# Attention pairs in eight slots: the steps of one turn taken from four different pairs

## The chip, the cores and the metric

The kernel runs on one core of a Trainium2 chip. Its metric is the device time of one execution in microseconds (us); for the kernel before, the median of three timed runs is 537.44 us (534.42 to 538.1).

## What is computed

Attention over 8 batches, 12 heads, 448 positions and 64 dimensions per head feeds a mixture of 8 experts, in which each expert takes at most 80 tokens:

```python
scores = scale * np.matmul(q, k.transpose(0, 1, 3, 2))
scores = np.where(mask, -1000000000.0, scores)          # causal
attn = np.exp(scores - np.max(scores, axis=-1, keepdims=True))
attn = attn / (np.sum(attn, axis=-1, keepdims=True) + 1e-09)
x = np.matmul(attn, v)                                  # -> rows of 768
logits = x @ w_gate; expert_idx = np.argmax(logits, axis=1)
for e in range(8):
    tok_idx = ...    # the 80 tokens of e with the largest gate weight
    out[tok_idx] = gate_w[tok_idx, None] * (np.maximum(x[tok_idx] @ w1[e], 0.0) @ w2[e])
```

## The kernel before, in words

**Pairs.** The attention runs over 48 pairs of heads, six to a batch. A pair's queries are cut into seven tiles (t = 0 to 6) of 64 queries for each of the two heads, one head in the lower 64 partitions and one in the upper. Tile t meets 64(t+1) keys. For a pair the kernel does, in this order:

- *scores*: two groups of TensorE (PE) matmuls (`products`, L355) into PSUM tiles `sp`. Group s0 holds tile 6 (one bank) and tiles 5 and 0 (a second bank); s1 holds tiles 4 and 1, 3 and 2. There are three `sp` banks, so four banks a pair go round three buffers.
- *softmax* of each tile (`softmax`, L358): the maximum, one VectorE (DVE) instruction that also scales and masks (`ns`, `nb`, L362), called m6, m5, ... below; and the exponential on ScalarE (ACT) into `prob` (L365), called e6, e5, ...
- *transposes*: two groups (`transpose_groups`, L379) of 16 PE instructions, t0 and t1, into the one two-bank PSUM tile `tp`, each with an ACT copy of that tile into `PT` (L384), c0 and c1. Since there is one `tp` buffer, t1 waits for c0 and the next t0 waits for c1. Group 0 reads all seven tiles of the pair, so t0 waits for the last exponential.
- *values*: 32 PE matmuls over four chunks of keys (`values_group`, L405) into the one `xp` bank, then a DVE copy into `xu` (L411).

**The order.** Everything in the attention is issued in the order that the program writes (`tc.manual_schedule()`, L891), and each engine works through its own instructions in that order. The loop of L911 gives each pair i eight slots. Slot by slot it puts the scores and softmax of pair i, the transposes of pair i-1 and the values of pair i-2 (`SCORES`, `TURNS`, `VALUES`, `READ` and `SOFT`, L27 to L28). On PE a turn so reads s0, t0, s1, t1, values; on ACT e6 e5 e0, c0, e4 e1 e3 e2, c1; on DVE the seven maxima, then the copy to `xu`.

**Batch steps.** When six pairs are done, the batch's other work is spread over the slots of later pairs by tables of slot numbers (`ROWS0`, `ROWS1`, `STEPS`, `batch_plan`, L871): transposes of the result rows (`rt`, L505) with a DVE scaling (L524) and a DMA to `xs`, the gate product (`gp`, L457), its transposes (`lp`), and the selection of each expert's best 80 tokens (`selt`, `rn`, `rl`, `cp`, `gt`, `tn` on PE, `less`, `lt`, `rm`, `rr` on DVE). Batch 6 has a table of its own (`EARLY`), and the last batch runs in `TAIL` (L39), after the pairs. These PE steps take PSUM from `ps_m`, two banks under one tag.

After the tail the experts run (L1255 on). The SP queue loads q and k half a batch ahead (three pairs), loads v, writes zeros to the output and loads the first expert weights in slots 1, 4 and 7.

Of the kernel before, what the change touches and what calls it, by code (L numbers as in the profile page):

```python
# [7 lines left out]
F32 = mybir.dt.float32  # L8
# [9 lines left out]
P = 128  # L18
# [4 lines left out]
TILES = 7  # L23
# [3 lines left out]
SCORES, TURNS, VALUES, READ = (0, 2), (1, 4), 5, 6  # L27
SOFT = {0: [6], 1: [5, 0], 2: [4], 3: [1, 3], 4: [2]}  # L28
# [11 lines left out]
u ta ya v0 tb yb v1 turned vy guard invert placed w gp0 wy close piece gp1 gs  # L40
# [8 lines left out]
def attention_then_moe(  # L49
# [13 lines left out]
    B, _, NP, S = qT.shape  # L63
# [5 lines left out]
    NT = (S + P - 1) // P  # L69
# [16 lines left out]
    apool = att.enter_context(tc.tile_pool(name="att", bufs=2))  # L86
# [36 lines left out]
    WIDTH = [QB * (t + 1) for t in range(TILES)]  # L123
# [210 lines left out]
    def scores_groups(pr, n):  # L334
# [32 lines left out]
        return products, softmax  # L367
# [482 lines left out]
    pairs = []  # L850
# [40 lines left out]
    with tc.manual_schedule():  # L891
# [18 lines left out]
        parts = []  # L910
        for i, pr in enumerate(pairs):  # L911
# [12 lines left out]
            products, softmax = scores_groups(pr, i)  # L924
            turns = transpose_groups(pairs[i - 1]) if i else []
            values = values_group(pairs[i - 2]) if i >= 2 else None
            for k in range(SLOTS):
                if k in SCORES:
                    products(SCORES.index(k))
                if turns and k in TURNS:  # L930
                    turns[TURNS.index(k)][0]()
                if values and k == VALUES:
                    values[0]()
                for t in SOFT.get(k, []):
                    softmax(t)
                if turns and k in TURNS:
                    turns[TURNS.index(k)][1]()
                if values and k == READ:
                    values[1]()
                for f in plan.pop(i * SLOTS + k, []):  # L940
                    f()

                if i == n - PH and k == 4 and len(wload) >= WBUF and not parts:
                    load_piece()

                if i > 4 and k in (1, 4, 7):
                    if not parts and len(wload) < WBUF:
                        parts = piece_parts()
                    if parts:
                        parts.pop(0)()  # L950
                    elif zdone[0] < N:
                        zero_rows()
# [25 lines left out]
        steps["u"] = lambda: None  # L978
# [357 lines left out]
```

## Time and profile before

| what | value |
| --- | --- |
| median of three runs | 537.44 us |
| the profiled execution | 536.23 us |
| its span, first to last instruction | 534.5 us |
| attention, from the first scores to the last transposes | 4.6 to 386 us |
| tail of the last batch and start of the experts | 386 to 425 us |
| experts | 425 to 534.5 us |
| busy: PE, PE weight loads, ACT, DVE | 454.5, 356.9, 372.2, 355.7 us |
| mean granted TensorE clock | 0.972 |

The profile gives busy time per engine, the granted clock of TensorE (1.0 is 2.4 GHz, 0.5 is 1.2 GHz), who waited for whom, and the chain of waits: the work that ended last, followed back step by step to whatever released it. In the attention the same picture repeats with every batch of six pairs, about 48.5 us, so a batch and a single pair are the units to read.

### The profile page before, as it was taken

The page shows a single profiled execution, that of the slowest core. Times are in us where ns is not written, and L with a number is a line of the kernel's source. Part 1 is how long each engine was busy: PE and PEld are TensorE (multiplying, and loading weights), DVE is VectorE, ACT ScalarE, POOL GpSimd, SP SyncE. Part 2 cuts the span into 40 slices and gives each one's busy share as a digit, 9 for nine tenths or more (in the row PEclk, how much of TensorE's full clock was granted, in tenths as well). Part 3 has the DMA queues.
Part 4 walks back from the last instruction along what each step waited for, and adds up shares of the span by engine and source line. Part 5 has one row for each costly group of instructions (what it writes and reads, how often), then busy time and mean ns, then how long its engine had stood idle before and what let it go on. Part 6 is the DMA issues. An engine that isn't in the chain of part 4 may idle for free.

```text
span 534.5 us, 17567 instructions
## 1 busy us (share of the span) xinstructions
PE 454.5 (85%) x7093; PEld 356.9 (67%) x7093; DVE 355.7 (67%) x1224; ACT 372.2 (70%) x973; POOL 79.6 (15%) x211
## 2 busy tenths in 40 slices
PE   5778878798788888787987888788887999999995
PEld 2556556556566566565565656666664999999994
DVE  4455465576566656765765567567756499999883
ACT  5876776767756847667667486575757399988792
POOL 4201010101101010101011001101045014522001
PEclk9899899999999989999999999999999599999998
DMA  7416595375559345842745360426164599999931
GB/s 259 171 53 221 164 326 184 103 238 178 197 166 324 109 148 169 286 160 107 254 164 186 120 243 21 169 75 215 25 268 149 174 394 389 396 391 423 424 154 38
DMA packets 36529, 110.05 MB, mean 206 GB/s; under 512 B 4658, under 2 KB 22834, under 8 KB 33248
## 3 DMA queue, kind: packets, MB, share of 16 engines
q1 hardware_dynamic: 35248, 105.19, 54.7%
q0 software_dynamic: 1056, 3.51, 2.1%
q8 instruction: 55, 0.90, 0.7%
q10 hardware_dynamic: 144, 0.23, 0.1%
q14 instruction: 26, 0.21, 0.1%
HBM read 85.35 MB, written 23.99 MB: 205 GB/s over the span
## 4 chain that ended last, share of the span: by engine, by line
PE 66%; ACT 19%; DVE 8%; issue 4%; DMA 1%; POOLq 0%; DVEq 0%; ACTq 0%
PE xp L405 18%; ACT prob L365 11%; PE tp L379 10%; PE sp L355 9%; ACT PT L384 7%; PE rt L505 4%; PE hp L1131 4%; PE op L1131 3%; PE op L1139 3%; PE gp L457 2%; PE hp L1146 2%; PE hp L1143 2%; PE hp L1145 2%; PE op L1141 1%; DVE xu L411 1%
## 5 line engine op out<-in xcount | busy, mean ns | idle before, releaser
L365 ACT ACTIVATE prob<-ns,nb 128x448 f32<-128x448 f32 (+6 forms) x336 | 167.0, 499 | 119.8 <-DVE nb L362 119.8
L362 DVE CUSTOM_DVE_ANT_0 ns<-sp,mask 128x448 f32<-128x448 f32 (+6 forms) x336 | 130.9, 420 | 67.4 <-PE sp L355 32.8
L379 PE MATMUL tp<-ident,prob 64*128 64x64 f32 x1536 | 69.4, 231 | 58.2 <-ACT PT L384 57.9
L355 PE MATMUL sp<-qk 64*64 64x256 f32 (+6 forms) x1344 | 107.5, 401 | 4.9 <-DMA qk<-k_t 4.6
L379 PEld LDWEIGHTS tp<-ident,prob 64*128 64x128 f32 x1536 | 56.1, 140 | 78.5 <-ACT PT L384 69.9
L405 PE MATMUL xp<-PT,vt 128*64 128x64 f32 (+3 forms) x1536 | 99.3, 285 | 0.0
L384 ACT COPY PT<-tp 128x1024 f32<-128x1024 f32 x96 | 95.1, 991 | 2.0 <-PE tp L379 2.0
L1059 DVE SCALAR_TENSOR_TENSOR wl<-wraw,wh 128x768 f16<-128x768 f32 (+1 forms) x91 | 91.9, 1070 | 3.0 <-ACT wh L1074 2.9
L405 PEld LDWEIGHTS xp<-PT,vt 128*64 128x64 f32 x1536 | 82.9, 142 | 13.4 <-issue 2.1
L355 PEld LDWEIGHTS sp<-qk 64*64 64x64 f32 x1344 | 57.7, 136 | 44.5 <-issue 24.7
L1074 ACT ACTIVATE wh<-wraw 128x768 f16<-128x768 f32 (+1 forms) x91 | 78.9, 929 | 6.2 <-DMA xs<-xrl 1.9
L411 DVE COPY xu<-xp 128x448 f32<-128x448 f32 x48 | 30.0, 624 | 68.3 <-PE xp L405 68.3
L365 ACT ACTIVATION_READ_ACCUMULATOR prob<-ns,nb 128x1 f32 x336 | 63.2, 188 | 0.0
L1146 PEld LDWEIGHTS <-wl 128*128 128x128 f16 x362 | 36.6, 101 | 1.4 <-DVE wl L1059 1.4
L1143 PEld LDWEIGHTS <-wh 128*128 128x128 f16 x362 | 37.0, 102 | 0.2 <-issue 0.2
L1145 PEld LDWEIGHTS <-wh 128*128 128x128 f16 x362 | 36.8, 102 | 0.0
L1146 PE MATMUL hp<-xh,wl 128*128 128x80 f16 x320 | 36.3, 205 | 0.1
L1143 PE MATMUL hp<-xh,wh 128*128 128x80 f16 x320 | 36.4, 205 | 0.0
L1145 PE MATMUL hp<-xl,wh 128*128 128x80 f16 x320 | 36.4, 205 | 0.0
L524 DVE TENSOR_TENSOR xr<-rt,norm 128x384 f32<-128x384 f32 (+1 forms) x56 | 30.3, 549 | 3.1 <-issue 1.9
L505 PE MATMUL rt<-ident,xu 128*128 128x128 f32 x192 | 31.7, 289 | 0.0
L1139 PE MATMUL op<-hh,wh 128*128 128x160 f16 x264 | 29.5, 234 | 0.0
(160 smaller groups left out, 550.8 us busy)
## 6 DMA issues: line engine op xcount, KB each, us to landing
wraw<-w SPq DMA_DIRECT2D x25, 1536.0 KB, 12.4
out<-mask SPq DMA_DIRECT2D x56, 192.0 KB, 3.9
qk<-q_t SPq DMA_DIRECT2D x15, 672.0 KB, 4.4
qk<-k_t SPq DMA_DIRECT2D x15, 672.0 KB, 6.5
vt<-v_t SPq DMA_DIRECT2D x16, 576.0 KB, 7.7
xs<-xr SPq DMA_DIRECT2D x42, 192.0 KB, 1.9
wraw<-w SPq DMA_DIRECT2D x30, 256.0 KB, 6.5
wraw<-w SPq DMA_DIRECT2D x16, 192.0 KB, 4.3
```

Source lines behind the costliest of these rows:

```text
L355: nc.tensor.matmul(pr.sp[t][to], st["q"][rows, p, t * QB:(t + 1) * QB], st["k"][rows, p, 0:WIDTH[t]], start=True, stop=True)
L362: nc.vector.tensor_tensor_reduce(out=ns[:, 0:w], in0=pr.sp[t], in1=mask[:, S - w:S], scale=-1.0 / 8.0, scalar=HUGE, op0=ALU.add, op1=ALU.m ...
L365: nc.scalar.activation(pr.P[:, OFF[t]:OFF[t] + w], ns[:, 0:w], AF.Exp, bias=nb, scale=-1.0, accum_out=pr.sums[:, pr.p * TILES + t:pr.p * T ...
L379: nc.tensor.transpose(tp[:, r, at:at + QB], pr.P[rows, off:off + P], ident[rows, rows])
L384: (nc.scalar.copy if how == "a" else nc.vector.tensor_copy)(pr.PT[:, g], pr.tp)
L405: nc.tensor.matmul(xp[rows, x0 * QB:x1 * QB], st["vt"][:, c, p * P + j * DH:p * P + (j + 1) * DH], pr.PT[:, g, 1 - j if crossed else j, at ...
L505: nc.tensor.transpose(tp[:, i, :], bt.xu[:, g * NH + i, whole_tile(t)], ident)
L1059: return nc.vector.scalar_tensor_tensor(out=l, in0=src, scalar=SW, in1=h, op0=ALU.mult, op1=ALU.subtract)
L1074: nc.scalar.activation(h, src, AF.Copy, scale=SW)
L1143: nc.tensor.matmul(o, wh[:, ws], ah[:, c, :], start=(x == 0 and i % per == 0), stop=False, skip_group_check=True)
L1145: nc.tensor.matmul(o, wh[:, ws], al[:, c, :], start=False, stop=False, skip_group_check=True)
L1146: nc.tensor.matmul(o, wl[:, ws], ah[:, c, :], start=False, stop=(x == n - 1), skip_group_check=True)
```

## The change

Each slot now has its own list of steps, and a turn works on four pairs at once: scores and softmax of pair i, transposes of pair i-1, the first chunk of the values of pair i-2 (`va`), and the other three chunks of the values of pair i-3 (`vb`) with its copy to `xu`. The maximum and the exponential of a tile are separate steps. `ns` gets four buffers for three, `nb` six for four. The numbers of `ROWS0`, `ROWS1` and `STEPS` now fall, with few exceptions, in slots 2 and 7 where they are PE work (the gap before t0 and the gap after t1), and the instruction that reads a PE result in the slot behind. `EARLY`, for batch 6, keeps its numbers. The tail gets the `vb` of the third pair from the end.

```diff
-SCORES, TURNS, VALUES, READ = (0, 2), (1, 4), 5, 6
-SOFT = {0: [6], 1: [5, 0], 2: [4], 3: [1, 3], 4: [2]}
+CYCLE = ["s0", "vb m6", "m5 m0 xu", "t0 e6 e5 e0", "s1 c0", "va m4 m1 e4 e1", "t1 m3 m2", "c1 e3 e2"]
-ROWS0 = [4, 5, 7, 13]
-ROWS1 = [59, 62, 64, 65]
+ROWS0 = [7, 10, 15, 18]
+ROWS1 = [26, 31, 58, 63]
...
-u ta ya v0 tb yb v1 turned vy guard invert placed w gp0 wy close piece gp1 gs
+u ta ya v0 tb yb v1 turned uy vy guard invert placed w gp0 wy close piece gp1 gs
...
-        def softmax(t):
+        def masked(t):
             w = WIDTH[t]
-            ns = apool.tile([P, S], F32, name="ns", tag="ns", bufs=3)
-            nb = apool.tile([P, 1], F32, name="nb", tag="nb", bufs=4)
+            ns = apool.tile([P, S], F32, name="ns", tag="ns", bufs=4)
+            nb = apool.tile([P, 1], F32, name="nb", tag="nb", bufs=6)
+            pr.soft[t] = ns, nb
             nc.vector.tensor_tensor_reduce(
...
+        def raised(t):
+            w = WIDTH[t]
+            ns, nb = pr.soft.pop(t)
             nc.scalar.activation(pr.P[:, OFF[t]:OFF[t] + w], ns[:, 0:w], AF.Exp, bias=nb, scale=-1.0,
...
+            if i:
+                for x, (work, copy) in enumerate(transpose_groups(pairs[i - 1])):
+                    ops[f"t{x}"], ops[f"c{x}"] = work, copy
+            if i >= 2:
+                values.append(values_group(pairs[i - 2]))
+                ops["va"] = lambda: values[-1][0](range(0, 1))
+            if i >= 3:
+                ops["vb"], ops["xu"] = lambda: values[-2][0](range(1, NT)), lambda: values[-2][1]()
             for k in range(SLOTS):
...
+                for name in CYCLE[k].split():
+                    if name in ops:
+                        ops.pop(name)()
                 for f in plan.pop(i * SLOTS + k, []):
                     f()
...
-        steps["u"] = lambda: None
+        steps["u"], steps["uy"] = lambda: values[-1][0](range(1, NT)), values[-1][1]
```

On PE, in the first batch, before: from the second transposes of one turn to the scores of the next (`tp` with `prob0` is t1, the seven `xp` rows are one pair's values).

```order
L379 MATMUL tp_460<-ident_88,prob0_99 128x64 x16
L405 MATMUL xp_482<-PT_283,vt0_109 64x128 x2
L405 MATMUL xp_482<-PT_283,vt0_109 64x256 x2
L405 MATMUL xp_482<-PT_283,vt0_109 64x64 x2
L405 MATMUL xp_482<-PT_283,vt0_109 64x128 x2
L405 MATMUL xp_482<-PT_283,vt0_109 64x192 x2
L405 MATMUL xp_482<-PT_283,vt0_109 64x128 x2
L405 MATMUL xp_482<-PT_283,vt0_109 64x64 x4
L355 MATMUL sp_501<-qk1_114 64x448 x2
L355 MATMUL sp_502<-qk1_114 64x384 x2
L355 MATMUL sp_502<-qk1_114 64x64 x2
L379 MATMUL tp_513<-ident_88,prob1_104 128x64 x16
```

The same stretch of PE in the changed kernel, from t1 of one turn to t0 of the next.

```order
L385 MATMUL tp_463<-ident_88,prob0_99 128x64 x16
L354 MATMUL sp_490<-qk1_114 64x448 x2
L354 MATMUL sp_491<-qk1_114 64x384 x2
L354 MATMUL sp_491<-qk1_114 64x64 x2
L411 MATMUL xp_448<-PT_283,vt0_109 64x128 x2
L411 MATMUL xp_448<-PT_283,vt0_109 64x192 x2
L411 MATMUL xp_448<-PT_283,vt0_109 64x128 x2
L411 MATMUL xp_448<-PT_283,vt0_109 64x64 x4
L385 MATMUL tp_518<-ident_88,prob1_104 128x64 x16
```

The scores s0 now come straight after t1 and the rest of the values after s0; the three first `xp` rows (chunk 0) stand before t1.

On ACT, in the first batch, before: one turn's exponentials by their width (448 is e6, 192 is e2) and the two copies.

```order
L365 ACTIVATE prob0_99,sums_153<-ns_317,nb_318 128x64
L384 COPY PT_283<-tp_296 128x1024
L365 ACTIVATE prob0_99,sums_153<-ns_332,nb_333 128x320
L365 ACTIVATE prob0_99,sums_153<-ns_336,nb_337 128x128
L365 ACTIVATE prob0_99,sums_153<-ns_340,nb_341 128x256
L365 ACTIVATE prob0_99,sums_153<-ns_366,nb_367 128x192
L384 COPY PT_283<-tp_349 128x1024
```

The same turn of ACT in the changed kernel.

```order
L371 ACTIVATE prob0_99,sums_153<-ns_298,nb_299 128x64
L390 COPY PT_283<-tp_301 128x1024
L371 ACTIVATE prob0_99,sums_153<-ns_344,nb_345 128x320
L371 ACTIVATE prob0_99,sums_153<-ns_347,nb_348 128x128
L390 COPY PT_283<-tp_352 128x1024
L371 ACTIVATE prob0_99,sums_153<-ns_369,nb_370 128x256
L371 ACTIVATE prob0_99,sums_153<-ns_372,nb_373 128x192
```

The second copy moved ahead of the last two exponentials; nothing was added to ACT.

On PE, around a batch's gate product `gp`, before: row transposes `rt` stand on either side of t0, and `gp` between s1 and t1.

```order
L505 MATMUL rt<-ident,xu 128x128 x3
L379 MATMUL tp<-ident,prob_104 128x64 x16
L505 MATMUL rt<-ident,xu 128x128 x3
L355 MATMUL sp<-qk_113 64x320 x2
L355 MATMUL sp<-qk_113 64x256 x2
L355 MATMUL sp<-qk_113 64x128 x2
L355 MATMUL sp<-qk_113 64x192 x2
L457 MATMUL gp<-xu,wgd 32x448 x6
L379 MATMUL tp<-ident,prob_104 128x64 x16
```

The same place of PE in the changed kernel, from t1 to t0.

```order
L385 MATMUL tp<-ident,prob_99 128x64 x16
L511 MATMUL rt<-ident,xu 128x128 x6
L354 MATMUL sp<-qk_113 64x448 x2
L354 MATMUL sp<-qk_113 64x384 x2
L354 MATMUL sp<-qk_113 64x64 x2
L411 MATMUL xp<-PT,vt_111 64x128 x2
L411 MATMUL xp<-PT,vt_111 64x192 x2
L411 MATMUL xp<-PT,vt_111 64x128 x2
L411 MATMUL xp<-PT,vt_111 64x64 x4
L511 MATMUL rt<-ident,xu 128x128 x3
L463 MATMUL gp<-xu,wgd 32x448 x6
L385 MATMUL tp<-ident,prob_104 128x64 x16
```

The batch steps moved into the two gaps: six `rt` instructions behind t1, and `rt` and `gp` between the values and t0.

## Rows read from the trace of the kernel before

**Rows 1.** The page's first line, and the chain that ended last, by engine.

```profile
span 534.5 us, 17567 instructions
PE 66%; ACT 19%; DVE 8%; issue 4%; DMA 1%; POOLq 0%; DVEq 0%; ACTq 0%
```

**Rows 2.** Busy time of the engines in stretches of the span: the stretch, its length, then busy us (and instructions) of PE, PE weight loads, DVE, ACT and POOL, the granted clock, the DMA share and GB/s. First one pair of the first batch, which has no batch steps beside it; then the turns of batches 1 to 7.

```profile
35.84:42.83 6.99, 5.34 (x96) 4.07 (x93) 3.47 (x15) 5.36 (x17) 0.00 (x0) 1.00 0.43 150
...
43.00:91.20 48.20, 39.29 (x606) 28.22 (x602) 27.91 (x119) 32.99 (x99) 3.20 (x16) 0.96 0.62 211
91.20:139.40 48.20, 40.07 (x629) 28.95 (x627) 30.63 (x134) 33.10 (x99) 4.10 (x21) 1.00 0.57 190
139.40:188.00 48.60, 40.47 (x640) 29.31 (x636) 31.36 (x136) 33.10 (x99) 4.30 (x22) 1.00 0.59 195
188.00:238.20 50.20, 42.07 (x639) 30.59 (x635) 31.36 (x136) 33.09 (x99) 4.27 (x22) 0.97 0.53 183
238.20:286.80 48.60, 40.47 (x639) 29.31 (x635) 31.36 (x136) 33.10 (x99) 4.31 (x22) 1.00 0.54 181
286.80:337.00 50.20, 42.07 (x640) 30.55 (x638) 31.46 (x136) 33.11 (x99) 4.30 (x22) 0.97 0.44 153
337.00:386.00 49.00, 41.90 (x648) 30.28 (x647) 33.38 (x143) 33.23 (x99) 4.64 (x23) 1.00 0.29 103
```

**Rows 3.** The chain of waits over one pair of the first batch, in order of time: start, us on the chain, what (the pieces of 0.02 to 0.04 us called "issue" are left out).

```profile
35.91 0.92 PE sp L355 x8
36.83 0.66 PE tp L379 x16
...
37.52 0.09 DVE nb L362
...
37.64 0.65 ACT prob L365
...
38.30 1.02 ACT prob L365 x4
39.33 0.90 ACT PT L384
...
40.28 0.71 PE tp L379 x16
40.99 1.91 PE xp L405 x32
42.90 0.48 PE sp L355
```

**Rows 4.** Instructions of that same pair in order of time: start, us, engine, line, what, and in brackets the idle time before it with its releaser. On ACT: e6, c0, e4 and c1.

```profile
37.64 0.67 ACT L365 ACTIVATE prob<-ns,nb 128x448 f32<-128x448 f32 x1 [1.63 <-DVE nb L362]
...
39.23 0.99 ACT L384 COPY PT<-tp 128x1024 f32<-128x1024 f32 x1
...
40.13 0.56 ACT L365 ACTIVATE prob<-ns,nb 128x320 f32<-128x320 f32 x1
...
42.00 0.99 ACT L384 COPY PT<-tp 128x1024 f32<-128x1024 f32 x1
```

**Rows 5.** The chain of waits over the pair in which batch 3's gate product runs; all of its pieces are PE (s0, a row transpose, ..., s1, the gate product, ..., the values).

```profile
206.29 0.92 PE sp L355 x8
...
208.81 0.91 PE sp L355 x12
209.71 1.65 PE gp L457 x12
...
212.00 1.93 PE xp L405 x32
```

**Rows 6.** Who waited for whom in the turns of batch 3 (139.4 to 188 us): waiter, releaser, us in total, times, longest.

```profile
ACT prob L365 <- DVE nb L362: 15.3, 7, 3.0
...
PE tp L379 <- ACT PT L384: 7.3, 5, 1.9
```

**Rows 7.** Two stretches of 2 us in the fourth batch, columns as in Rows 2.

```profile
190.00:192.00 2.00, 0.80 (x16) 0.39 (x10) 1.65 (x10) 2.00 (x8) 0.29 (x2) 1.00 0.65 236
...
194.00:196.00 2.00, 2.00 (x18) 1.57 (x17) 0.51 (x1) 1.38 (x4) 0.00 (x0) 0.50 0.27 98
```

**Rows 8.** The values of two pairs, as in Rows 4: one that starts just before 194 us, and the next pair's.

```profile
193.78 3.62 PE L405 MATMUL xp<-PT,vt 128*64 128x128 f32 x32
...
203.50 1.98 PE L405 MATMUL xp<-PT,vt 128*64 128x128 f32 x32
```

**Rows 9.** The end of the last pair's turn, as in Rows 4: the last values in the loop, the last exponential, and the first transposes of the tail.

```profile
384.29 1.98 PE L405 MATMUL xp<-PT,vt 128*64 128x128 f32 x32
...
384.60 0.44 ACT L365 ACTIVATE prob<-ns,nb 128x192 f32<-128x192 f32 x1
...
386.20 0.71 PE L379 MATMUL tp<-ident,prob 64*128 64x64 f32 x16
```

**Rows 10.** Two groups of DVE batch steps in the turns of batch 3: line, engine, what, count, busy us, mean ns of one, idle before.

```profile
L661 DVE SCALAR_TENSOR_TENSOR less<-rn,ggw,before 128x512 bf16<-128x512 f32 (+3 forms) x4 | 2.2, 544 | 0.0
...
L541 DVE TENSOR_REDUCE logit<-lg 128x32 f32<-128x384 f32 x1 | 0.6, 553 | 0.0
```

**Rows 11.** Loads of k and v: issues, KB each, median us from issue to landing.

```profile
qk<-k_t SPq DMA_DIRECT2D x15, 672.0 KB, 6.5
vt<-v_t SPq DMA_DIRECT2D x16, 576.0 KB, 7.7
```

More of the change, by code (lines that the diff above doesn't have):

```diff
@@ L31 @@
 ROWGAP = 1
-ROWS0 = [4, 5, 7, 13]
-ROWS1 = [59, 62, 64, 65]
-STEPS = {'gp': 18, 'gs': 18, 'lp': 21, 'lg': 22, 'logit': 23, 'shifted': 25, 'chosen': 26, 'sums': 27, 'one_hot': 28, 'weight': 28, 'weighted': 31, 'columns': 30, 'parts': 33, 'r0t': 32, 'r0c': 33, 'r1t': 34, 'r1c': 35, 'rl': 36, 'lt': 36, 'c3w': 38, 'c3l': 39, 'cp': 40, 'ro': 41, 'c2w': 41, 'c2l': 43, 'c1w': 43, 'c1l': 44, 'c0w': 46, 'c0l': 46, 'gt': 47, 'earlier': 51, 'own': 47, 'rank': 51, 'places': 63, 'places_more': 66, 'rr': 73, 'tn': 77, 'tab': 78, 'rp': 80, 'row': 81, 'rr_more': 75}
+ROWS0 = [7, 10, 15, 18]
+ROWS1 = [26, 31, 58, 63]
+STEPS = {'gp': 18, 'gs': 19, 'lp': 23, 'lg': 24, 'logit': 25, 'shifted': 26, 'chosen': 27, 'sums': 28, 'one_hot': 29, 'weight': 29, 'columns': 31, 'weighted': 32, 'parts': 33, 'r0t': 34, 'r0c': 35, 'r1t': 39, 'r1c': 40, 'rl': 39, 'lt': 40, 'c3w': 42, 'c3l': 43, 'cp': 42, 'ro': 43, 'c2w': 47, 'c2l': 48, 'c1w': 47, 'c1l': 49, 'c0w': 50, 'c0l': 51, 'gt': 55, 'own': 56, 'earlier': 57, 'rank': 58, 'places': 63, 'places_more': 66, 'rr': 66, 'rr_more': 68, 'tn': 74, 'tab': 75, 'rp': 79, 'row': 80}
 EARLY = {'gp': 18, 'gs': 18, 'lp': 21, 'lg': 21, 'logit': 22, 'shifted': 24, 'chosen': 26, 'sums': 27, 'one_hot': 28, 'weight': 29, 'weighted': 31, 'columns': 30, 'parts': 32, 'r0t': 33, 'r0c': 33, 'r1t': 34, 'r1c': 34, 'rl': 35, 'lt': 35, 'c3w': 36, 'c3l': 37, 'cp': 38, 'ro': 39, 'c2w': 39, 'c2l': 40, 'c1w': 40, 'c1l': 41, 'c0w': 41, 'c0l': 42, 'places': 43, 'places_more': 43, 'gt': 44, 'earlier': 44, 'own': 44, 'rank': 46, 'rr': 46, 'tn': 48, 'tab': 50, 'rp': 51, 'row': 52, 'rr_more': 46}
@@ L356, in products @@
                                          start=True, stop=True)
-        def softmax(t):
+        pr.soft = {}
+        def masked(t):
             w = WIDTH[t]
-            ns = apool.tile([P, S], F32, name="ns", tag="ns", bufs=3)
-            nb = apool.tile([P, 1], F32, name="nb", tag="nb", bufs=4)
+            ns = apool.tile([P, S], F32, name="ns", tag="ns", bufs=4)
+            nb = apool.tile([P, 1], F32, name="nb", tag="nb", bufs=6)
+            pr.soft[t] = ns, nb
             nc.vector.tensor_tensor_reduce(
@@ L364, in softmax @@
                 accum_out=nb)
+        def raised(t):
+            w = WIDTH[t]
+            ns, nb = pr.soft.pop(t)
             nc.scalar.activation(pr.P[:, OFF[t]:OFF[t] + w], ns[:, 0:w], AF.Exp, bias=nb, scale=-1.0,
                                  accum_out=pr.sums[:, pr.p * TILES + t:pr.p * TILES + t + 1])
-        return products, softmax
+        return products, masked, raised
     def transpose_groups(pr):
@@ L909, in attention_then_moe @@
             later_on(LATE + x * SLOTS, [f])
-        parts = []
+        parts, values = [], []
         for i, pr in enumerate(pairs):
@@ L923, in attention_then_moe @@
                 load_values(h)
-            products, softmax = scores_groups(pr, i)
-            turns = transpose_groups(pairs[i - 1]) if i else []
-            values = values_group(pairs[i - 2]) if i >= 2 else None
-            for k in range(SLOTS):
[L928 to L939, printed above, removed]
+            products, masked, raised = scores_groups(pr, i)
+            ops = {"s0": lambda: products(0), "s1": lambda: products(1)}
+            for t in range(TILES):
+                ops[f"m{t}"], ops[f"e{t}"] = lambda t=t: masked(t), lambda t=t: raised(t)
+            if i:
[6 more added lines that the diff above has]
+                ops["vb"], ops["xu"] = lambda: values[-2][0](range(1, NT)), lambda: values[-2][1]()
+            for k in range(SLOTS):
+                for name in CYCLE[k].split():
+                    if name in ops:
+                        ops.pop(name)()
                 for f in plan.pop(i * SLOTS + k, []):
```

## The prediction

> **What bounds the kernel now.** I read the page's first lines, then busy time by stretches, then the chain of waits over one pair, then the instructions of that pair, and last the list of waits.
>
> The page says that two thirds of the chain are PE and a fifth ACT, and that no transfer is on it to speak of [rows 1]. By stretches, a turn of six pairs takes 48.2 to 50.2 us, of which PE is busy about 40.5 us (42.07 in the two long ones), ACT 33.1 and DVE 31.4 [rows 2]. So no engine is full: PE stands idle some 8 us in each of seven such turns. The pair without batch steps shows it best: 6.99 us long, with PE busy 5.34 and ACT 5.36 [rows 2].
>
> The chain over that pair names the loop [rows 3]: s0 0.92, then 0.81 up to the start of the first exponential (36.83 to 37.64; the chain names t0, but the maximum of tile 6 runs then), exponentials of tiles 6, 5 and 0 0.65 and 1.04, copy c0 0.90, transposes t1 0.71, values 1.91, and s0 of the next pair. With the small gaps that is 42.90 - 35.91 = 6.99 us, the whole period. Both engines take turns in one ring: t1 waits for c0, because there is one `tp` tile; s0 of the next pair stands in PE's order behind t1 and the values; and ACT waits 1.63 us for the maximum that needs those scores [rows 4]. The list of waits repeats it: in one batch ACT waits 15.3 us for the maxima, PE 7.3 us for the copy [rows 6].
>
> **The change part by part.**
>
> *The values leave the ring.* Arithmetic is neither added nor removed: the same 32 matmuls, seven maxima, seven exponentials and two copies a pair. What changes is what stands between c0 and the next first exponential. Now s0 follows t1 at once, and the values lie elsewhere: chunk 0 before t1, while c0 runs, and chunks 1 to 3 after s0, while the maxima and e6, e5, e0 run. So the ring loses the 1.91 us of the values: 6.99 - 1.91 = 5.08 us, less than either engine's own work.
>
> *What is late next.* In the plain pair, ACT's own order. From c1 to the next e6 nothing should wait: e6 to c0 takes 1.69 us (37.64 to 39.33 [rows 3]), c0 0.90, the four exponentials 42.00 - 40.13 = 1.87 [rows 4], c1 0.90, which with 0.09 of gaps is 5.45 us. A second ring, c0 0.94, t1 0.71, c1 0.94, e3 and e2 0.93 (half of 1.87), e6 to e0 1.69, comes to 5.21; a third, t0 0.66, s1 0.91 [rows 5], chunk 0 0.84 (448 of 1024 columns of 1.91), t1 0.71, c1 0.94, e3 and e2 0.93, to 4.99. All four lengths lie within 0.5 us, so I take the longest, 5.45, for a plain pair: 1.54 less than 6.99. The first batch has four such pairs, at 7.0 or a little more: 4 x 1.54 = 6.2 us.
>
> *The pairs with batch steps.* From the second batch on, PE has more: 40.47 / 6 = 6.75 us a pair [rows 2], against 5.45 for ACT's order. There PE should be the bound, if its steps stand where they hold up nobody. The steps in slot 7 lie in the 5.08 ring (between t1 and s0), those in slot 2 do not (the values and t0 follow only c0 and e2, long done), and both lie in PE's sum, so a ring with the steps of slot 7 stays below PE's own work. That PE can run dense is seen in the pair with the gate product: its chain is PE alone from 206.29 to 213.93 [rows 5]. For changes of hands, and for DVE steps that stand ahead of a maximum, I add 0.3 us a pair: three changes of engine at the 0.04 of the chain, and an estimated 0.2 for the steps. Bounds: 0 at best, as in that dense pair; at worst half of DVE's batch work, 31.36 - 6 x 3.47 = 10.5 us a batch [rows 2], lands on the path, 0.9 us a pair.
>
> *The clock.* In the turn that begins at 188 us the granted clock is 0.50 from 194 to 196, at 1.2 GHz, after a stretch in which PE was busy 0.80 of 2 us [rows 7]; the values there take 3.62 us for 1.98 [rows 8], 1.6 us lost, which is the 42.07 against 40.47. Three turns have such a dip (clock 0.96, 0.97 and 0.97 [rows 2]). With PE's waits gone I count all three as gone. The Trainium skill, "TensorE: Matmul & The Clock Gate", section "HAM oscillation — how this bites in real kernels", says that idle gaps let the clock drop and that denser work keeps it up; by that the dips go, as counted, and if they stayed the sum would be 4.8 us higher. The trace agrees with it as far as rows 7 go.
>
> *The sum.* Floor of each turn: PE busy, less 1.6 where there is a dip, plus 6 x 0.3 = 1.8 [rows 2].
> Batch 1: 39.29 - 1.6 + 1.8 = 39.5 for 48.2: -8.7.
> Batch 2: 41.9 for 48.2: -6.3.
> Batches 3 and 5: 42.3 for 48.6: -6.3 each.
> Batches 4 and 6: 42.3 for 50.2: -7.9 each.
> Batch 7: 41.90 + 1.8 = 43.7 for 49.0: -5.3.
> That is -48.7, and with the first batch -54.9 us.
>
> *What costs nothing, and its cover.* The tail gets the rest of pair 45's values, 1.91 x 576/1024 = 1.07 us on PE. Before, the tail's first transposes at 386.20 came right behind a whole pair of values that began at 384.29, while the last exponential had begun at 384.60 [rows 9]. Now c1 and two exponentials, 1.9 us, stand between t1 and those transposes and cover it; without the cover it costs 1.07. The later copy to `xu` (0.6 us) lies beside the row transposes; the gate product stays at slot 18, behind it in DVE's order. More buffers for `ns` and `nb` cost no time; they could be worth a little, 0 to 0.2 us a pair, already inside the 0.3. Loads of q, k and v are still issued three pairs ahead or 2.6 pairs ahead of use, now about 20 and 17 us for landings of 6.5 and 7.7 us [rows 11]. On SP the writes of the rows move by three to five slots; none now stands just ahead of a load of the next half, since they follow slots 8, 11, 16, 19, 27, 32, 59 and 64 and the loads come ahead of slots 0 and 24. The experts after 425 us are untouched.
>
> The profiled execution took 536.2 us: 536.2 - 54.9 = 481.3. It was 1.2 us under the median of the runs, so I predict 482 us.
>
> **The rivals.**
>
> *DVE holds up the maxima (506 us).* Batch steps stand in DVE's order beside the maxima: the gate's sum of 553 ns falls in slot 1 between m6 and m5, and the four comparisons of 544 ns [rows 10] fall around slots 0, 1 and 3. If half of the 10.5 us a batch delays an exponential and through c0 the next transposes, 5.3 us a batch stand in place of my 1.8: 7 x 3.5 = 24.5 us more, 506. For it: the engines' orders are strict here, and the plain rings leave only 0.1 to 0.5 us. Against: PE's sum exceeds ACT's by 1.3 us a pair, which absorbs a delay of that size.
>
> *PE's floor is lower (464 us).* The busy rows count each group to its modelled end; the pieces of the chain for the plain pair, 0.92 + 0.66 + 0.91 + 0.71 + 1.91 = 5.11, are 0.23 less than its 5.34. With that and no loss at hand-overs, 42 x 0.53 = 22 us less at most; some of each gives 464. Against: the plain pairs are ACT's, and the splitting of the values adds a change of group. The Trainium skill, "Perfetto Trace Analysis", section "Identifying the Most-Contended Engine", says matmul busy time is no good measure of PE's headroom and points to weight-load busy time. By that measure PE is busy 29.3 of 48.6 us, ACT's 33.1 plus 1.8 would bound a batch, and the time would be near 430; the dense pair of rows 5, PE alone for 7.6 us, speaks against so low a floor.
>
> *The clock turns against it (562 us), the case on the slow side.* Place: the attention's turns. If PE's denser fp32 work were given 1.2 GHz in places, a pair there would cost another 6.75 us; from nine pairs of 48 on (55 / 6.75 = 8.1) the kernel is slower than before, and with twelve it takes 482 + 80 = 562. Against: the half clock in the trace follows idleness, and the dense turns have 1.00 [rows 2, 7].
>
> *The change does not do what it says (537 us).* The wait moves instead of going: t1 still waits for c0 in the one `tp` tile, and if t0 came to wait for e2 as long as ACT now waits for m6, the period would stay near 7. That needs 1.9 us more in the third ring than its rows sum to.
>
> **How the numbers follow.** My case, 469 (no loss a pair) to 497 (0.7 a pair): 0.68. DVE: 0.17. The lower floor: 0.06. No change: 0.05. The clock: 0.04. The likeliest gives 482 us. The range goes from 465, inside the lower floor, to 506, the DVE case's own value, which leaves out half of that case and the last two. A measurement tells about 1% from no change: faster by more 0.91, within 0.05, slower 0.04.
>
> **What would show it.** In the changed trace: plain pairs of the first batch at 5.4 to 5.6 us; turns of six pairs at 41.5 to 43 us with PE busy above 93% of them; ACT's wait for the maxima down from 15.3 us a batch, and what is left of it hidden behind a busy PE; no stretch of half clock between 40 and 330 us; the first transposes of the tail near 331 us. The prediction is wrong if PE still idles more than 1 us a pair there, and the releaser tells which rival holds: a maximum (DVE), the copy, the last exponential, or a transfer.

## The result, and the profile after

The changed kernel takes 453.5 us (median of four runs, 453.43 to 453.82) against 537.0 us: ratio 0.8452, interval 0.8420 to 0.8483. That is 83.6 us less. The prediction was 482 us, with 465 as its lower end: the side was right, the size was not, and the time fell below the range. The profiled execution took 453.45 us. A run more than 1.5% above the fastest of its kernel stays out of the ratios; there are two such below, 471.9 us (the values whole) and 463.3 us (the first better order).

The page of the changed kernel, to be held against [rows 1]; its first line, the engines' busy time and share, the clock in 40 slices, and the chain that ended last by engine:

```profile
span 451.7 us, 17614 instructions
...
PE 434.4 (96%) x7093; PEld 345.1 (76%) x7093; DVE 347.3 (77%) x1224; ACT 377.7 (84%) x973; POOL 82.9 (18%) x211
...
PEclk9999999999999999999999999999999999999998
...
PE 84%; ACT 9%; DVE 2%; DMA 2%; issue 2%; POOLq 0%; DVEq 0%; ACTq 0%
```

PE holds 84% of the chain, not 66%; ACT's share is halved; and the clock has no slice below 9 until the last. The stretches that answer to [rows 2], with the same columns: one plain pair of the first batch (c1 to c1), then the turns of batches 1 to 3 and 7 (those of 4 to 6 take 39.3, 39.3 and 39.2 us).

```profile
24.70:30.00 5.30, 5.29 (x99) 4.04 (x96) 3.12 (x15) 5.30 (x18) 0.00 (x0) 1.00 0.49 145
...
35.20:73.20 38.00, 37.57 (x601) 27.30 (x597) 25.70 (x114) 34.17 (x102) 2.99 (x15) 1.00 0.78 264
73.20:112.20 39.00, 39.00 (x632) 28.91 (x631) 29.54 (x135) 34.06 (x100) 4.07 (x20) 1.00 0.73 241
112.20:151.40 39.20, 39.20 (x636) 29.17 (x635) 30.43 (x136) 34.05 (x100) 4.26 (x21) 1.00 0.71 242
...
269.20:312.90 43.70, 42.84 (x679) 31.60 (x678) 34.74 (x151) 35.64 (x104) 5.20 (x24) 1.00 0.45 150
```

In batches 2 and 3 the length and PE's busy time are the same number, and so they are in 4 to 6: PE is busy from the first instant of a turn to the last. DVE and ACT are not full, and the clock is 1.00 throughout, so the three dips of [rows 2, 7] are gone. The last row reaches past the turn of batch 7 into the tail (below). The chain over one dense pair of batch 3 (start, us, what), which answers to [rows 3]:

```profile
118.31 0.92 PE sp L354 x8
119.23 1.14 PE xp L411 x20
120.38 0.80 PE rt L511 x6
121.18 0.64 PE tp L385 x16
121.83 0.90 PE sp L354 x12
122.73 0.93 PE xp L411 x12
123.66 0.65 PE tp L385 x16
124.31 0.80 PE rt L511 x6
125.11 0.92 PE sp L354 x8
```

The ring is gone: s0, three chunks of an older pair's values, row transposes, t0, s1, the first chunk of the next values, t1, row transposes, s0, and no wait between them. The copies and maxima lie beside. What is left of the waits in [rows 6] for batch 3 (waiter, releaser, us in total, times, longest):

```profile
ACT prob L371 <- DVE nb L364: 4.0, 11, 0.5
```

ACT's wait for a maximum fell from 15.3 us to 4.0, and PE's wait for the copy is not in the list any more.

Where the 83 us went, by stretches of the two profiled executions (us from the span's start; the last values begin at 391.16 and 317.73, the first expert matmul at 412.58 and 336.68):

| stretch | before | after | difference |
|---|---|---|---|
| first scores to the last values | 386.6 | 313.05 | -73.55 |
| last values to the first expert matmul | 21.42 | 18.95 | -2.5 |
| first expert matmul to the end | 121.93 | 115.06 | -6.9 |

### The profile page after: what moved, and what is told of

It is laid out like the page before. It is cut to its first block, busy times and chain, and to the rows that moved or that the text cites. A ratio compares the mean times of both kernels' runs of the same rounds, so it can differ in the third digit from the quotient of the medians.

```text
span 451.7 us, 17614 instructions
## 1 busy us (share of the span) xinstructions
PE 434.4 (96%) x7093; PEld 345.1 (76%) x7093; DVE 347.3 (77%) x1224; ACT 377.7 (84%) x973; POOL 82.9 (18%) x211
## 4 chain that ended last, share of the span: by engine, by line
PE 84%; ACT 9%; DVE 2%; DMA 2%; issue 2%; POOLq 0%; DVEq 0%; ACTq 0%
PE xp L411 19%; PE sp L354 17%; PE tp L385 12%; PE rt L511 5%; ACT prob L371 5%; PE op L1137 4%; PE hp L1137 4%; PE op L1145 3%; PE gp L463 3%; PE hp L1152 3%; ACT PT L390 3%; PE hp L1151 3%; PE hp L1149 3%; PE op L1147 2%; PE rn L664 1%
## 5 line engine op out<-in xcount | busy, mean ns | idle before, releaser
L364 DVE CUSTOM_DVE_ANT_0 ns<-sp,mask 128x448 f32<-128x448 f32 (+6 forms) x336 | 124.8, 419 | 62.1 <-PE sp L354 44.0
L411 PE MATMUL xp<-PT,vt 128*64 128x64 f32 (+3 forms) x1536 | 105.1, 279 | 0.0
L354 PE MATMUL sp<-qk 64*64 64x256 f32 (+6 forms) x1344 | 97.3, 396 | 4.9 <-DMA qk<-k_t 4.7
L354 PEld LDWEIGHTS sp<-qk 64*64 64x64 f32 x1344 | 54.0, 134 | 39.9 <-issue 23.6
L1149 PEld LDWEIGHTS <-wh 128*128 128x128 f16 x362 | 36.4, 101 | 0.0
L1151 PEld LDWEIGHTS <-wh 128*128 128x128 f16 x362 | 36.2, 100 | 0.0
L1152 PE MATMUL hp<-xh,wl 128*128 128x80 f16 x320 | 35.2, 202 | 0.0
L1151 PE MATMUL hp<-xl,wh 128*128 128x80 f16 x320 | 35.2, 202 | 0.0
L1149 PE MATMUL hp<-xh,wh 128*128 128x80 f16 x320 | 35.2, 202 | 0.0
L1238 POOL DMA_INDIRECT out<-yo,idx x8 | 20.8, 2604 | 63.3 <-ACT yo L1235 59.1
L448 POOL COPY norm<-sums 64x12 f32<-64x12 f32 (+1 forms) x60 | 10.8, 193 | 116.4 <-DVE sums L431 114.8
```

The costliest lines, as they stand in the source:

```text
L354: nc.tensor.matmul(pr.sp[t][to], st["q"][rows, p, t * QB:(t + 1) * QB], st["k"][rows, p, 0:WIDTH[t]], start=True, stop=True)
L364: nc.vector.tensor_tensor_reduce(out=ns[:, 0:w], in0=pr.sp[t], in1=mask[:, S - w:S], scale=-1.0 / 8.0, scalar=HUGE, op0=ALU.add, op1=ALU.m ...
L411: nc.tensor.matmul(xp[rows, x0 * QB:x1 * QB], st["vt"][:, c, p * P + j * DH:p * P + (j + 1) * DH], pr.PT[:, g, 1 - j if crossed else j, at ...
L1149: nc.tensor.matmul(o, wh[:, ws], ah[:, c, :], start=(x == 0 and i % per == 0), stop=False, skip_group_check=True)
L1151: nc.tensor.matmul(o, wh[:, ws], al[:, c, :], start=False, stop=False, skip_group_check=True)
L1152: nc.tensor.matmul(o, wl[:, ws], ah[:, c, :], start=False, stop=(x == n - 1), skip_group_check=True)
```

## The experiments

My theory after the result: the values had closed a ring over PE, ACT and DVE; with them out of it, PE's own instructions bound every turn from the second batch on, and the steps in two gaps keep it so. The rivals: that the two tables, the split of the values, the place of c1 or the larger buffers did it; that ACT or DVE is as near to the bound; and, for the experts' 6.9 us, that something other than the clock gave them. Ratios are to the kernel before, run on the same chip (medians 536.0 to 538.2).

**The values back in the ring.** The rest stays as changed; the values of a pair are whole again and stand between t1 and the next s0.

```diff
-"s0", "vb m6", "m5 m0 xu", ..., "va m4 m1 e4 e1", "t1 m3 m2", "c1 e3 e2"
+"s0", "m6", "m5 m0", ..., "m4 m1 e4 e1", "t1 m3 m2", "c1 e3 e2 va xu"
```

> The changed kernel with one thing undone: the values of pair i-2 stand again whole on PE, between t1 and the next s0; ACT's order, the buffers and the slots of the batch steps stay as changed. Theory A (the values between c0 and the next maxima make the ring): a plain pair is back near 6.9 us (5.26 + 1.9 less what is hidden), a turn of six near 47 to 49 us for 39.25, the time 515 to 535 us. Theory B (the gain comes from putting the batch steps into the two gaps): most of the gain stays, a turn of 40 to 42 us, 455 to 475 us.

Measured: 521.2 us, ratio 0.9719 (0.9658 to 0.9780). First scores to last values takes 381.1 us. The chain over a plain pair of the first batch:

```profile
28.33 0.92 PE sp L354 x8
29.25 0.67 PE tp L385 x16
...
30.72 1.02 ACT prob L371 x4
31.74 0.90 ACT PT L390
...
32.69 0.71 PE tp L385 x16
33.40 1.91 PE xp L411 x32
35.31 0.80 PE sp L354 x3
```

It is [rows 3] again, piece for piece, and its period is again 35.31 - 28.33 = 6.98 us. So 521.2 - 453.5 = 67.7 of the 83.6 us hang on where the values stand, their split in two pieces included. Part of them is the clock's: the trace has seven stretches at half clock in this attention, the kernel before has four and the changed kernel none. Of two first pairs of a turn with the same instructions, one with such a stretch takes 9.43 us (89.47 to 98.90, clock 0.82) and one without 7.94 (186.32 to 194.26, clock 1.00); at 1.5 us each, an estimate, seven make some 10 of the 67.7. The tables, the order of ACT and the buffers together, with the values in the ring, gain 386.6 - 381.1 = 5.5 us in the attention, and would gain some 4.5 more without the three additional stretches; the rest of this kernel's lead over the one before lies behind the attention, where it takes 19.0 and 115.1 us, as the changed kernel does (the causes follow below).

**The old tables of batch steps in the new cycle.**

```diff
-ROWS0 = [7, 10, 15, 18];  ROWS1 = [26, 31, 58, 63];  STEPS = {..., 'r1t': 39, ..., 'gt': 55, ...}
+ROWS0 = [4, 5, 7, 13];  ROWS1 = [59, 62, 64, 65];  STEPS = {..., 'r1t': 34, ..., 'gt': 47, ...}
```

> The changed kernel with the batch steps back in the slots of the kernel before (both row tables and the step table); the turn of eight slots stays. Theory A: plain pairs stay at 5.26 us, PE stays nearly full and the steps only now and then delay a maximum: turns of 39.5 to 41.5 us, 455 to 470 us. Theory B: a turn of 44 us or more, 490 us or more.

Measured: 468.3 us, ratio 0.8733 (0.8665 to 0.8800). A turn (columns as in [rows 2]):

```profile
113.80:154.70 40.90, 40.25 (x639) 29.38 (x636) 30.62 (x136) 33.50 (x101) 4.29 (x22) 1.00 0.70 233
```

A turn takes 1.7 us more than 39.2, though the instructions are the same: PE waits 0.65 us of it, and the rest stands in its busy time, 40.25 for 39.20, as in the turns before. This is the profiled run, at 470.2 us. First scores to last values is 322.2 us in it, so the tables are worth 9 us there, about a ninth of the whole gain; of the other 7.6 us the experts make 6.5, 121.5 us for 115.06, at half clock again, and the tail most of the rest. The second run took 466.5 us at a mean clock of 0.997 for 0.981; it has no trace, so where its time went is open.

**The values whole, behind s0.** No chunk before t1.

```diff
-ops["va"] = lambda: values[-1][0](range(0, 1))
+pass
-ops["vb"], ... = lambda: values[-2][0](range(1, NT)), ...
+ops["vb"], ... = lambda: values[-2][0](), ...
```

> The changed kernel with the values of pair i-3 in one piece after s0, none before t1. On PE a pair's two pieces take 0.93 + 1.14 = 2.07 us in the dense turns and the whole 1.91, so PE has 0.16 us less a pair. Theory A with a tight t1 (t1 waits for c0, and only s1's 0.90 us lies between t0 and t1): c0 takes 0.94 from t0's end, so t1 waits 0.05 to 0.15 us a pair and the two nearly cancel: 450 to 456 us. If the split is what keeps t1 from waiting (c0 itself begins late, behind e0): 0.4 us or more a pair, 470 us or more.

Measured: 465.7 us (three runs, 464.5 to 467.5; with the fourth, 471.9, the median is 466.6), ratio 0.8689 (0.8626 to 0.8752): I missed by 10 us. A turn, and a piece of its chain:

```profile
116.60:157.10 40.50, 38.77 (x636) 28.67 (x635) 30.54 (x137) 33.92 (x101) 4.26 (x21) 1.00 0.69 235
```

```profile
126.88 0.66 PE tp L385 x16
127.54 0.02 issue
127.56 1.02 ACT PT L390
...
128.63 0.71 PE tp L385 x16
```

Whole values need less of PE (38.77 for 39.20), but PE idles 1.73 us of the turn: between t0 and t1 stands s1 alone (0.90), and c0 with its hand-overs takes 128.63 - 127.54 = 1.09. The plain pairs take 5.4 to 6.3 us, the longest of them partly at half clock. The chunk ahead of t1 is the cover of c0, as the change's first part supposed; splitting costs a little PE and saves more.

**c1 behind the exponentials it follows.**

```diff
-"c1 e3 e2"
+"e3 e2 c1"
```

> The changed kernel with the second copy c1 back behind the last two exponentials on ACT. Theory A: the order on ACT matters little once the values are out of the ring; t0 waits for c1 now, e3 and e2 0.93 and c1 0.94 stand behind t1 as before in the other order, so the ring has the same length: within 3 us of 453. Theory C (c1's place is what frees PE): t0 waits longer for the tp tile, 0.5 us or more a pair, 475 us or more.

Measured: 455.4 us (two runs, 456.1 and 454.6), ratio 0.8490 (0.8435 to 0.8546). The turns are as long as in the changed kernel (39.27). Nearly all that the profiled run loses, 2.6 us, lies in one place of the first batch (stretches as in [rows 7]):

```profile
13.00:16.20 3.20, 1.64 (x30) 1.07 (x30) 1.88 (x11) 3.20 (x11) 2.97 (x9) 0.91 0.02 5
16.20:21.70 5.50, 5.50 (x63) 4.13 (x64) 1.58 (x12) 4.40 (x15) 0.76 (x5) 0.50 0.27 73
```

PE was busy 1.64 of 3.2 us (2.03 in the changed kernel, whose clock stays at 1.00 there), and the pair, from 14.07 to 21.68, ran mostly at half clock: 7.61 us for 5.25. So in the turns c1's place is worth nothing; whether it also brought the half clock in the first batch, these two runs do not show.

**Each engine's work made larger.** Three kernels repeat some of the changed kernel's instructions: the row transposes on PE, the exponential of tile 1 on ACT, the maximum of tile 1 on DVE.

```diff
-for i in range(NH):                       # PE
+for i in list(range(NH)) * (1 if ps_x else 2):
+for _ in range(2 if t == 1 else 1):       # ACT: the exponential; DVE: the maximum
```

> The changed kernel with each row transpose of the attention done twice into the same place: 56 groups of three, 0.37 to 0.48 us a group, some 23 us more PE work and nothing else. Theory A (the turns are bound by PE's own work, no waits left): the time rises by nearly all of it, 470 to 478 us. If another engine or a ring set the pace: under 465.

> The changed kernel with the exponential of tile 1 done twice: 48 times 0.40 us, 19 us more ACT work. Theory A: in the turns with batch steps ACT has 5 us in 39.2 to spare and takes 2.4 more, so only the plain pairs of the first batch (4 x 0.4) and a few tight places pay: 455 to 460 us. If ACT sets the pace: 470 us or more.

> The changed kernel with the maximum of tile 1 done twice: 48 times 0.2 to 0.3 us, some 11 us more DVE work in front of m3, m2 and of the later maxima. Theory A: hidden, 453 to 456 us. The rival of the prediction (DVE's steps hold up the maxima, and through them PE): 460 us or more.

Measured: PE 471.8 us, ratio 0.8790 (0.8715 to 0.8865); ACT 459.6, ratio 0.8563 (0.8490 to 0.8636); DVE 453.9, ratio 0.8462 (0.8426 to 0.8499). On PE, the group of the transposes in the changed kernel and in the one that repeats them (line, engine, what, count, busy us, mean ns):

```profile
L511 PE MATMUL rt<-ident,xu 128*128 128x128 f32 x192 | 31.1, 284 | 0.0
```

```profile
L511 PE MATMUL rt<-ident,xu 128*128 128x128 f32 x360 | 49.4, 279 | 0.0
```

49.4 - 31.1 = 18.3 us of busy time came in, and 471.8 - 453.5 = 18.3 us came out: all of it, which is what a bound looks like. On ACT some 19 us came in and 6.1 out: in the plain pairs, 0.53 us each, and in the first pair of a turn, where ACT was as full as PE. That pair of batch 3, in the changed kernel and in the one with the longer ACT work (columns as in [rows 2]):

```profile
112.24:118.31 6.07, 6.07 (x111) 4.65 (x112) 4.89 (x24) 6.04 (x18) 1.83 (x10) 1.00 1.00 362
```

```profile
115.70:122.20 6.50, 6.17 (x111) 4.68 (x114) 4.93 (x24) 6.43 (x22) 1.83 (x10) 1.00 1.01 371
```

On DVE some 13 us came in, and the time rose by 0.4. So the rival that DVE holds up the maxima is false, and ACT is the second bound, in those pairs alone.

**Smaller buffers.** `ns` and `nb` as they were.

```diff
-name="ns", bufs=4   name="nb", bufs=6
+name="ns", bufs=3   name="nb", bufs=4
```

> The changed kernel with three buffers for the masked scores and four for the maxima, as before. The prediction gave them 0 to 0.2 us a pair: 453 to 463 us. With three buffers m4 waits for e3 of the pair before and m6 for e1, both some us earlier in the turn, so near the lower end: 453 to 456.

Measured: 453.6 us (453.49 to 453.68), ratio 0.8456 (0.8427 to 0.8486). The difference to 453.5 is within the runs' own spread: the buffers are worth nothing here.

**The clock at the experts.** Between the attention's end and the experts PE waits for a gathered row tile `xg`, and filler matmuls (`*20` in the tail's order) keep it busy. One kernel is the kernel before with more of them, the other the changed kernel with fewer.

```diff
 before:  -rank rr tn tab *20     +rank rr tn tab *36
 after:   -rank rr tn tab *20     +rank rr tn tab *8
```

> The kernel before with 36 for 20 of the idle-filling matmuls at the end of its tail, so that PE works on until the gathered tokens land (20 of them ended 2.7 us earlier). The attention is untouched. Theory D (about 6.5 us of the gain lie in the experts' start, which ran at half clock after PE had idled in the gather, 121.9 us from the first expert matmul to the end for 115.1): 528 to 532 us for 536. Theory A alone (all of the gain is in the attention): 535 to 538.

> The changed kernel with 8 for 20 of those matmuls, so that PE idles some 2.5 us before the tokens land. Theory D: the experts start at half clock again, 457 to 461 us for 453.5. If the clock in the experts has another cause: 453 to 454.

Measured: the kernel before with more filler 531.0 us (ten runs), ratio 0.9906 (0.9873 to 0.9939); the changed kernel with less 458.05 us, ratio 0.8532 (0.8476 to 0.8588), 4.6 more than with `*20`. The stretches around the first expert matmuls (columns as in [rows 2]), in the order before, before with more filler, changed kernel with less:

```profile
409.20:411.90 2.70, 0.01 (x1) 0.00 (x0) 0.61 (x1) 2.29 (x3) 2.09 (x3) 1.00 0.48 85
413.00:423.00 10.00, 10.00 (x49) 10.00 (x49) 6.08 (x6) 2.94 (x5) 0.84 (x1) 0.50 0.52 169
```

```profile
409.20:413.20 4.00, 3.94 (x22) 1.86 (x20) 1.52 (x2) 2.82 (x3) 3.01 (x3) 1.00 0.44 104
414.00:424.00 10.00, 10.00 (x174) 10.00 (x175) 8.00 (x10) 6.30 (x12) 2.10 (x2) 1.00 0.87 285
```

```profile
333.50:336.00 2.50, 0.03 (x1) 0.00 (x0) 2.50 (x3) 2.50 (x4) 1.89 (x3) 1.00 0.18 38
338.00:348.00 10.00, 10.00 (x58) 10.00 (x58) 5.41 (x5) 2.52 (x5) 0.78 (x2) 0.50 0.97 348
```

In the two kernels where PE idled there, for 2.7 and 2.5 us, the next 10 us of experts ran at half clock; where filler covered the wait, they ran at full clock, and the experts' part is 115.1 us instead of 121.9 and 119.9. So the 6.9 us of the last row of my table are the clock's, and no instruction of the new order gives them: PE's wait for the gather was covered in the run after and not in the run before.

**Better orders.** Two kernels try to have both the cheaper whole values and the cover of c0. In the first the values are whole as above, and the batch steps of slot 7 move ahead of t1, to cover c0.

```diff
-ROWS0 = [7, 10, 15, 18];  ROWS1 = [26, 31, 58, 63];  'lp': 23, 'r1t': 39, 'rl': 39, 'c2w': 47, 'c1w': 47, 'gt': 55, 'rp': 79
+ROWS0 = [7, 10, 13, 18];  ROWS1 = [26, 29, 58, 61];  'lp': 21, 'r1t': 37, 'rl': 37, 'c2w': 45, 'c1w': 45, 'gt': 53, 'rp': 77
```

> The values in one piece after s0, as in the unsplit run, and the batch steps that stood in the gap after t1 put before t1 (one row transpose stays), where PE waits for c0. Theory: the pieces of the values cost 0.16 us a pair of PE more than the whole, and the steps fill the wait that the unsplit run showed: turns of 38.3 to 39.2 us, 447 to 453 us, faster than the changed kernel. If t1's lateness itself matters (c1 and the last exponentials start later, and the next t0 with them): turns of 40 us, 457 us or more.

Measured: 456.1 us (five runs, 455.9 to 459.2; with the sixth, the profiled one at 463.3, the median is 457.3), ratio 0.8522 (0.8492 to 0.8551), so not the 447 to 453 I hoped for. Its six pairs of a turn take 6.61, 6.65, 7.62, 6.48, 5.84 and 5.86 us, against 6.07, 6.79, 7.78, 6.63, 5.99 and 6.01 in the changed kernel: 0.14 to 0.16 less in five of them, which is what the split costs PE, and 0.54 more in the first, where PE waits 0.50 us for c0. A turn is 0.2 us shorter for it (39.1). The first and last batches, with few steps, lose as well, and from the first scores to the last values it takes 2.3 us more than the changed kernel.

The second takes each where it is better: whole values and the moved steps in pairs 2 to 6 of a turn of batches 1 to 6, the split elsewhere, and four more filler matmuls.

```diff
+had, split = split, pr.p == 0 or i < NP or i >= n - NP
+if split:
     ops["va"] = lambda: values[-1][0](range(0, 1))
-tn tab *20
+tn tab *24
```

> The values in one piece, with the batch steps before t1, only in those turns of a batch in which the run before this had gained 0.14 to 0.16 us a pair (the second to the sixth); the first turn of each batch, which had lost 0.54 us there, and the first and last batch keep the split values, and gt its gap. Also 24 for 20 of the idle-filling matmuls at the end of the tail (0 to 0.6 us dearer, and PE does not idle if the gather is late). Theory A: turns of 38.4 to 38.6 us for 39.25, six of them: 448.5 to 451 us, faster than the changed kernel. If splitting has another use (t1 late in the turns behind the first): 453 us or more.

Measured: 451.8 us (six runs, in two groups, 449.9 to 450.3 and 453.3 to 453.9), ratio 0.8392 (0.8360 to 0.8423). A turn:

```profile
110.10:148.70 38.60, 38.60 (x641) 28.88 (x637) 30.28 (x137) 33.75 (x100) 4.29 (x21) 1.00 0.73 247
```

0.6 us a turn less than 39.2, with PE again full; first scores to last values takes 309.1 us, 4 less than after. Its median is the lowest of the kernels I ran. By the two ratios its lead over the changed kernel is 0.7%, with intervals that touch (0.8423 and 0.8420), and the two groups are 3.4 us apart, so the lead is not clear of noise. What sets the groups I did not measure in each run; the profiled run, at 453.4 us, had a late gather (last section), and in it the tail took 20.2 us for 18.95 and the experts 117.65 for 115.06, at full clock: what the attention gained was lost again behind it.

## Why the prediction was wrong

The mechanism held at each point where it was stated: the values leave the ring, PE becomes the bound in the turns with batch steps and ACT's order in the plain pairs, the dips of the clock go, the tail's extra values are covered. The sum was 27.9 us too long (481.3 against 453.45), in these terms:

- **"For changes of hands ... I add 0.3 us a pair."** This is the step that failed first. In the five turns of batches 2 to 6 it is 5 x 1.8 = 9.0 us, and it measured nothing: PE's busy time equals the turn's length. I had named the dense chain of [rows 5] as the bound "0 at best" and then chosen a value without a row behind it. With the old tables a loss of this kind is there, 1.7 us a turn; it is the moved steps that take it away.
- **"Floor of each turn: PE busy."** The floor was too high by 6.1 us over the same five turns: 211.1 was predicted for them, of which 9.0 is the term above, and 196.0 was measured, so 15.1 - 9.0. The instructions are the same, and their busy time was 40.07 and 40.47 a turn without the dips [rows 2] against 39.20. The difference is in how busy time is counted. Summed group by group, each to its modelled end, PE's work in the turn of batch 3 is 43.5 us before and after (43.55 and 43.47). But where one group follows another at once, it begins before the modelled end of the first, and such overlaps count once: 3.03 us before, when 8.1 us of waits stood between groups, and 4.13 after, when none did. Pieces of the chain show it: t1 ahead of the values takes 0.71 [rows 3], in the dense chain after 0.65. The rival "PE's floor is lower" had this right, with 0.23 us a pair, and I gave it 0.06. Its cap, "42 x 0.53 = 22 us less", and its time of 464, some of each, still stood 10.5 us too high, since it touches neither the first batch nor what lies behind the attention (1.5 + 2.5 + 6.9).
- **Batch 1 and the plain pairs.** Batch 1 was to take 39.5 us and took 38.0: the same two terms (1.8, and 37.7 of PE for 37.57), less 0.4 us in which PE waits there. The first batch gained 7.75 us, not 6.2, for two reasons. One is a fourth stretch at half clock in the kernel before, which the prediction did not count: its third pair takes 7.70 us (columns as in [rows 2]; 0.50 from 16.4 to 19.8), 0.7 more than the plain 6.99.

```profile
14.17:21.87 7.70, 6.57 (x96) 5.00 (x93) 2.93 (x16) 6.69 (x23) 2.88 (x9) 0.78 0.21 61
```

  The other: a plain pair takes 5.26 us, not 5.45. In the changed kernel the chain over these pairs is ACT's alone, and ACT has no gap in them. One period of it (256 keys wide is e3, with e2, e6, e5 and e0 behind it; then c0, e4 with e1, c1 and the next e3):

```profile
25.72 0.53 ACT L371 ACTIVATE prob<-ns,nb 128x256 f32<-128x256 f32 x1
...
28.24 1.02 ACT L390 COPY PT<-tp 128x1024 f32<-128x1024 f32 x1
29.14 0.59 ACT L371 ACTIVATE prob<-ns,nb 128x320 f32<-128x320 f32 x1
...
30.08 1.02 ACT L390 COPY PT<-tp 128x1024 f32<-128x1024 f32 x1
30.98 0.53 ACT L371 ACTIVATE prob<-ns,nb 128x256 f32<-128x256 f32 x1
```

  The order is as named, and so is the bound; the sum was misread. By the starts in [rows 4], e6 to c0 is 39.23 - 37.64 = 1.59, c0 40.13 - 39.23 = 0.90, the four exponentials 1.87, and with 0.90 for c1 that is 5.26, the period measured. The prediction took e6 to c0 from the chain, where c0's piece begins only at 39.33 [rows 3], 0.10 late, and added 0.09 for gaps that ACT's own rows do not have. The added work on ACT, 0.53 us a pair, confirms that ACT sets these pairs, although PE is busy in them too (5.29 of 5.30).
- **Batch 7** was to take 43.7 us for 49.0. The row above, also 43.7, is no match, for it reaches into the tail: its PE time holds the tail's part of pair 45's values and six of its first transposes.

```profile
310.63 1.21 PE L411 MATMUL xp<-PT,vt 128*64 128x128 f32 x20
312.01 0.40 PE L385 MATMUL tp<-ident,prob 64*128 64x64 f32 x6 [0.17 <-ACT PT L390]
312.96 0.53 PE L385 MATMUL tp<-ident,prob 64*128 64x64 f32 x10 [0.54 <-ACT prob L371]
```

  The turn itself, from its first scores at 269.24 to the end of its t1 at 310.6, takes 41.4 us: the same two terms. From those scores to the tail's last values it is 54.2 us before (336.99 to 391.16) and 48.5 after (269.24 to 317.73), 5.7 less, against 5.3 in the forecast: most of what the turn saves beyond its 5.3 goes again at the tail's start, to the moved values (1.21) and PE's two waits (0.17 and 0.54).
- **The tail.** Predicted without change; it took 2.5 us less, which is PE's wait for the gathered tile in front of the first expert transposes: 2.73 us before, 0.18 after (rows in the last section). The extra values of pair 45 are covered, as supposed: behind them PE still waits for c1 and for the last exponential. The tail's first transposes came at 312 us, not near 331: that is the attention's miss again.
- **"The experts after 425 us are untouched."** Their instructions are, their clock was not: 6.9 us. The half clock was in the trace of before, at 413 to 423 us, ahead of the 425 of this sentence, in a stretch for which the sum has no term; I did not look there, as the change touches nothing in it. The rule of the Trainium skill, "TensorE: Matmul & The Clock Gate", section "HAM oscillation — how this bites in real kernels", that idle gaps let the clock drop, which the prediction applied to the attention, applies here too, and these runs agree with it: waits of 2.73 and 2.53 us, then a clock of 0.50.

The terms 15.1, 1.5 (batch 1), 1.5 (first batch), 0.4 (batch 7 to the last values), 2.5 (tail) and 6.9 make the 27.9. The last two, 9.4 us, are no merit of the change as far as these runs show: they hang on when one gather starts (last section), and that they came is luck.

The other rivals. DVE: false, as its added work shows. The clock on the slow side: false, 1.00 in every turn, transposes and fp32 products among them. No change: false; in the turns t0 does not wait for e2. The rule of the Trainium skill, "Perfetto Trace Analysis", section "Identifying the Most-Contended Engine", by which the prediction came to a side remark of 430 us with ACT as the bound, does not hold here, and the measurement decides: weight loads are busy 29.2 of 39.2 us in a turn, and yet 18.3 us more work for PE, nearly all of it in such turns, made the time 18.3 us longer.

## What to carry to other kernels

Where two engines take turns in a ring and neither is full, look for work in the ring that nothing in it needs soon, and move that out: here one group of 1.91 us a pair gave 68 of 84 us. What was moved still has to stand where it helps: in one piece it would have given back 12 of them, and batch steps in the wrong gaps cost 9. Then put the bound engine's floor together from chain pieces of a stretch in which that engine runs alone, not from its busy time in stretches full of waits, and add no loss per hand-over for which there is no row. And a saving ahead of a stretch shifts what meets there: look at the clock of stretches that the change does not touch, too.

## What the runs showed of the hardware

Whether the experts start at half clock went here with the order of two instructions on different engines. The first gather `xg` runs on POOL beside DVE's long `wl` operations. Instructions around it (start, us, engine, line, what, and the idle time ahead with its releaser), in the kernel before and after:

```profile
406.32 3.50 DVE L1059 SCALAR_TENSOR_TENSOR wl<-wraw,wh 128x1024 f16<-128x1024 f32 x3
...
407.57 2.06 POOL L1091 DMA_INDIRECT xg<-xs,idx  x1 [4.67 <-DVE wl L1059]
...
411.94 0.67 PE L1109 MATMUL xtp<-ident,xg 80*128 80x80 f32 x6 [2.73 <-DMA xg<-xs,idx]
```

```profile
332.67 1.08 POOL L1097 DMA_INDIRECT xg<-xs,idx  x1 [3.20 <-DVE gws L849]
...
332.88 3.56 DVE L1065 SCALAR_TENSOR_TENSOR wl<-wraw,wh 128x1024 f16<-128x1024 f32 x3
...
335.95 0.60 PE L1115 MATMUL xtp<-ident,xg 80*128 80x80 f32 x6 [0.18 <-DMA xg<-xs,idx]
```

Where the gather begins 0.21 us ahead of `wl`, it takes 1.08 us. Before, it began only when the first of the three `wl` had ended, 1.25 us after that began, and took 2.06 us. In the mixed order of the last experiment it began 0.13 us behind `wl` (329.07 and 328.94) and took 2.04. The other traces sort the same way: in the nine in which it begins ahead of `wl`, by 0.20 to 0.22 us, it takes 1.08; in the five in which it begins behind, by 0.10 to 1.25 us, 1.31 to 2.08. Before, PE then waits 2.73 us, where it waits 0.18 after, and the half clock follows. It also followed waits of 1.52 us (old tables) and 1.45 us (first better order), and did not follow one of 0.76 (the last experiment). The Trainium skill, "SBUF — State Buffer", section "Who interferes with whom", says that a DVE operation with two inputs in SBUF shares ports with GpSimd's reads, and that the order of issue decides who is blocked; the gather's times agree with it. The first `wl` takes 1.14 us to the start of the next in both orders. No run here took `wl` away, so the link between the two is read from the order of times, not shown by an edit; that the wait behind it costs the clock is shown by the two filler kernels. No edit here aims at this order, and what sets which of the two comes first stays open.
